# A window-attention and gated-expert kernel: the output product of tiles 3 to 8 by seven block products as well

## Chip, core and metric

The kernel runs on one core of one Trainium2 chip. The metric is the device time of one execution in microseconds (us); the table below gives it as the median of three runs. Everything said of single instructions comes from one further execution, which the hardware profiler recorded. TensorE (PE) does the matmuls, VectorE (DVE) and ScalarE (ACT) work on PSUM and SBUF, GpSimd (POOL) on SBUF, and SyncE (SP) issues nearly all DMA transfers.

## What is computed

Attention over a window of 64 positions, and behind it a gated expert layer:

```python
scores = q @ k.T / sqrt(64), masked to 0 <= i - j < 64     # 8 batches, 8 heads, 576 positions, head size 64
x = (softmax(scores) @ v), heads side by side              # 4608 tokens x 512
xn = x / sqrt(mean(x*x) + 1e-6) * rms_g
g, val = xn @ w_gate, xn @ w_val                           # 512 -> 1536
out = (silu(g) * val) @ w_out                              # 1536 -> 512
```

All tensors are float32. To keep nearly that precision on TensorE, each operand of the expert layer is split into a high and a low half of 16 bits, and each product is three matmuls: high by high, high by low, low by high.

## The kernel before

The 4608 tokens are nine tiles of 512 (`TT`), t = 0 to 8. The hidden width of 1536 is six chunks c of 256 (`NC`, `WC`). Tiles 0 to 2 multiply plainly. From tile 3 (`FIRST7`) on the gate and value products of a chunk are made by a seven-product scheme (Strassen and Winograd's): tokens, features and columns are halved, and sums and differences of the quarters of the weights and of x are multiplied, seven block products in place of eight (`product`, L976). One block product is 12 matmuls of 128x256 (L992). The weight sums are made once by `prepare` (L910), are kept in DRAM (`sevens`), and are streamed back for each chunk by `load_sevens` (L968, L974) into one of three SBUF buffers, `wts[r % 3]`.

`seventh` (L1026) runs product p and hands the accumulator on: ACT copies it away (`snap`, L1007), DVE adds a kept copy (L1045, L1048, L1052), and `quad` (L1010) makes the gated values of one quarter: a tanh on ACT (L1016), two DVE operations on 128x256 (L1017, L1018). When both halves of a row of quarters are there, ACT writes the high half (L1023) and POOL, or DVE for the last chunk, the low half (L1024).

The output product of these tiles is plain: `chunk_out` (L1126) multiplies, for 128 tokens k and chunk c, six matmuls of 128x512 through `three` (L845 to L847). One such unit is an `out_unit`, 24 units make a tile, and `store` (L1133) scales the result of six units on ACT (L1135) and writes it out (L1148).

The order is written by hand in slots. A slot is one block product or one output unit on TensorE; a tile has `SHORT` = 66 slots, 42 products (places 7c + `PLACE[p]`) and 24 units, which begin at slot 42 and fill the free slots, two of them in the next tile. `at_slot(when, part)` puts any other work into the order at a fractional slot, and each engine and DMA queue runs its instructions strictly in that order. The attention of batch b runs during tile b - 1, up to tile 6, at the offsets `SCORES`, `VALUES` and so on: scores of a head pair on TensorE (L395), masks on DVE (L408), exponentials on ACT (L411), scaling on POOL (L366), a transposition through DRAM by SP (L374, L380) and DVE (L383), values on TensorE (L526). Normalising (L788) and the sums and splits of x (`combine`, L814) follow. Tiles 7 and 8 have no attention beside them.

From tile 1 on the eight PSUM banks are one pool: each new tile takes the next bank in turn (`any_bank`, L86).

Of the kernel before, what the change touches and what calls it, by code (L numbers as in the profile page):

```python
# [7 lines left out]

# [17 lines left out]
P = 128  # L26
# [14 lines left out]
LT0, LV0 = 1.4, 2.6  # L41
SCORES, VALUES = (-14, -4, 8, 21), (12, 22, 34, 47)
LOAD, MASK, EXP, SUM, SCALE, AWAY, BACK, TURN = -6, (0.3, 0.5), (1.3, 0.9), 9.7, 10, 12.5, 16, 22
ROOTS, FIRST, SECOND, PIECE = 50.5, 52.5, 61, 0.85
FIRST7 = 3
PLACE = {1: 0, 5: 2, 2: 3, 6: 4, 3: 6, 7: 8, 4: 12}
LONG, SHORT = 72, 66
PREP, PREP_EVERY, PREP_PIECE = 3, 9.6, 0.9
ST = 2 * NBLK * P - 32
NRB = B  # L50
S1, LK1, LV1, LQ1 = [-2, 1, 3, 6, 10, 12.5, 15.5, 19], 2.5, 6, 7
# [11 lines left out]
def tile_window_attention_moe(  # L63
# [22 lines left out]
    def any_bank(name):  # L86
        return shared["banks"].tile([P, TT], F32, tag="bank", name=name)
# [168 lines left out]
    def in_scale(c):  # L256
# [18 lines left out]
        nc.gpsimd.tensor_scalar(h_inv[:, c : c + 1], s[:, 1, 0:1], 2.0**-6, s[:, 1, 1:2], ALU.mult, ALU.mult)  # L275
# [137 lines left out]
    def scores_of_pair(n, qk, first):  # L413
# [121 lines left out]

    def attention(b):
# [21 lines left out]
        def moves(hp):  # L558
            n = b * NPAIR + hp

            def turned():
                p, m, _ = whole.pop(n)
                turn(p, m)
                soft[hp, 0] = soft[hp, 1] = p

            return (
                (SCALE, lambda: scale(whole[n][0], whole[n][2])),
                (AWAY, lambda: away(n, whole[n][0])),
                (BACK, lambda: back(n, whole[n][1])),
                (TURN, turned),  # L570
            )
# [4 lines left out]
        def values(hp, g, xp=None):  # L576
            n = b * NPAIR + hp
            vv = pairs[hp][1]
# [12 lines left out]
            nc.scalar.copy(xb[:, hp, a:z], xp[:, : z - a])  # L591
            if g == 0:
                return
# [4 lines left out]
        def squares(hp):  # L598
            xb, ssq = norm["x"], norm["ssq"]
            x2 = pairs[hp][0] if hp else ssq  # L600
            x2e = E("X2E", "a" * 8)[b * NPAIR + hp] if b < 2 else "a"
# [5 lines left out]
        def add(hp):  # L607
            ssq = norm["ssq"]
            if hp:
                e = nc.vector if (E('ADD', 'ppvppv')[3 * b + hp - 1] == 'v' if b < 2 else hp == NPAIR - 1) else nc.gpsimd  # L610
                e.tensor_tensor(ssq, ssq, pairs[hp][0], ALU.add)

        def roots():
            norm["r"] = inverse_roots(b, norm["ssq"])
# [33 lines left out]
    def at_slot(when, part):  # L648
        if when < 0:
            at_step(half_steps + when / 2, part)  # L650
        else:
            timed.append((when, len(timed), part))
            timed.sort(key=lambda e: e[:2])

    def attention_slots(b):
# [9 lines left out]
        def normal(piece, when):  # L665
            for i, part in enumerate(normal_parts(piece)):
                at_slot(when + PIECE * i, part)

        for hp in range(NPAIR):
            s, v = t0 + SCORES[hp], t0 + VALUES[hp]  # L670
            early_by = 14 if b == TB and hp < 2 else -LOAD
            at_slot(s - early_by, partial(load_queries, hp))
            at_slot(s - early_by, partial(load_keys, hp))
# [5 lines left out]
        at_slot(t0 + ROOTS, roots)  # L679
        at_slot(t0 + FIRST, partial(normal, 0, t0 + FIRST))  # L680
        at_slot(t0 + SECOND, partial(normal, 1, t0 + SECOND))

    def first_batch():
# [12 lines left out]
        LT, LV = [LT0] * 8, [LV0] * 8  # L696
# [28 lines left out]
    def inverse_roots(b, ssq):  # L725
# [13 lines left out]
        inverse_root(m, r, w, tot[:, :nst])  # L739
        return r  # L740
# [30 lines left out]
    def normalise(b, xb, r, piece):  # L771
# [104 lines left out]
    def group_in(t, c, i, m, bank):  # L876
# [17 lines left out]
        nc.vector.scalar_tensor_tensor(th, a, 2.0**-41, th, ALU.mult, ALU.mult)  # L894
# [11 lines left out]
    RIGHT = {1: "11", 2: "21", 5: "t1", 6: "t2", 3: "22", 7: "t3", 4: "t4"}  # L906
    sevens = [dram.tile([P, 14 * TT], F16, name=f"sevens{c}") for c in range(NC)]
    HT = TT // 2

    def prepare(c, i):  # L910
# [40 lines left out]
        def away(j):  # L951
            nc.sync.dma_start(out=out_of[:, 2 * TT * (2 * i + j) : 2 * TT * (2 * i + j + 1)], in_=halves[j])
# [6 lines left out]
    def block(p, i, j):  # L959

        if p in SUMS:
            return 2 * TT * (2 * i + j) + HT * SUMS[p]
        at = 8 * TT + 3 * TT * i
        return at + (2 * TT + HT * j if p == 4 else TT * j + HT * (p - 1))

    SUMS = {6: 0, 7: 1, 3: 2, 5: 3}

    def load_sevens(r):  # L968
# [3 lines left out]
        dst = wts[r % 3].rearrange("p i a n -> p (i a n)")  # L972
        for a, z in ((0, 8 * TT), (8 * TT, 14 * TT)):
            nc.sync.dma_start(out=dst[:, a:z], in_=sevens[r % NC][:, a:z])  # L974

    def product(t, c, p, acc, first):  # L976
# [3 lines left out]
        for i in range(2):  # L980
            ws = []
            for j in range(2):
                o = block(p, i, j)
                w = wt[4 * (r % 3) + o // 2048].rearrange("p a n -> p (a n)")
                ws.append(w[:, o % 2048 : o % 2048 + HT].rearrange("p (k f) -> p k f", k=2))
# [19 lines left out]
    def snap(src, t, c, p):  # L1005
        d = wt[11][:, 1, :].bitcast(F32) if p == 5 else late.tile([P, TT], F32, tag=f"s{p}", name=f"s{p}_{t}_{c}")
        nc.scalar.copy(d, src)  # L1007
        kept[c, p] = d

    def quad(t, c, i, half, acc):  # L1010

        if (c, "th", i) not in kept:
            kept[c, "th", i] = wk.tile([P, TT], F32, tag="t2k", name=f"th_{t}_{c}_{i}", bufs=T2K), []
        th, done = kept[c, "th", i]
        cols = th[:, half * HT : (half + 1) * HT]
        nc.scalar.activation(cols, acc[:, :HT], AF.Tanh, scale=th_scale[:, c : c + 1])  # L1016
        nc.vector.scalar_tensor_tensor(cols, cols, 1.0, acc[:, :HT], ALU.add, ALU.mult)  # L1017
        nc.vector.scalar_tensor_tensor(cols, acc[:, HT:], 2.0**-41, cols, ALU.mult, ALU.mult)  # L1018
        done.append(half)
        if len(done) == 2:  # L1020
            kept.pop((c, "th", i))
            hh, hl = hs[t, c][:, 0, i, :], hs[t, c][:, 1, i, :]
            nc.scalar.copy(hh, th)  # L1023
            (nc.vector if c == NC - 1 else nc.gpsimd).tensor_tensor(hl, th, hh, ALU.subtract)  # L1024

    def seventh(t, c, p):  # L1026

        if p == 1:
            hs[t, c] = wk.tile([P, 2, 2, TT], F16, tag="f4k", name=f"h_{t}_{c}", bufs=F4K)
# [6 lines left out]
        if p == 1:  # L1036
            kept[c, "x"] = acc
            snap(acc, t, c, 1)
        elif p == 5:
            kept[c, "w"] = acc  # L1040
            snap(acc, t, c, 5)
        elif p == 6:
            snap(acc, t, c, 6)
        elif p == 2:
            nc.vector.tensor_tensor(acc, acc, kept.pop((c, 1)), ALU.add)  # L1045
            quad(t, c, 0, 0, acc)
        elif p == 3:
            nc.vector.tensor_tensor(acc, acc, kept.pop((c, 6)), ALU.add)  # L1048
            quad(t, c, 0, 1, acc)
        elif p == 7:  # L1050
            w = kept[c, "w"]
            nc.vector.tensor_tensor(w, acc, kept.pop((c, 5)), ALU.add)  # L1052
            quad(t, c, 1, 1, w)
        else:
            quad(t, c, 1, 0, acc)
            load_sevens(NC * (t - FIRST7) + c + 3)
# [9 lines left out]
    def outs_of(t):  # L1066
        last = NC - 1
        order = [(0, c) for c in range(last)] + [(1, c) for c in range(last - 1)] + [(0, last), (1, last - 1), (1, last)]
        order += [(k, c) for k in range(2, TT // P) for c in range(NC)]
        return [(tile_start(t) + (NC + 1) * last + 7, t, k, c) for k, c in order]  # L1070
# [3 lines left out]
    def out_unit(t, k, c):  # L1074
        if t == NT - 1 and k == TT // P - 1:
            if c == 0:
                for e in range(2):
                    es = slice(e * DM // 2, (e + 1) * DM // 2)
                    po = any_bank(f"po_{t}_{k}_{e}")[:, es]
                    for c in range(NC):  # L1080
                        chunk_out(po, t, c, k, c == 0, c == NC - 1, es)
                    store(po, t, k, es)
            return
# [7 lines left out]
    def rest_of_tiles():  # L1091
# [5 lines left out]
        for t in range(1, FIRST7):  # L1097
            for c in range(NC):
# [5 lines left out]
                if t == FIRST7 - 1 and c % 2:  # L1104
                    at_slot(now, partial(load_sevens, c // 2))
# [200 lines left out]
```

## Time and profile before

| | |
|---|---|
| time, median of 3 runs | 1003.25 us (1003.04 to 1003.25) |
| profiled execution | 1004.02 us, of which 1002.1 us from the first to the last instruction |
| granted TensorE clock, mean | 0.986 |
| busy: PE, DVE, ACT, POOL | 971.0, 578.4, 498.9, 330.3 us |
| moved by DMA | 171.74 MB, mean 171 GB/s |

A group's row has the source line, the engine, the operation, what it writes and reads, the shapes and the count; then the busy time and the mean duration of one; then the idle time of the engine just before these instructions and what ended it. A row of the windows has the stretch, its length, and then the busy time of PE, of PE's weight loads (PEld), DVE, ACT and POOL with the counts of instructions, the granted clock, the share of DMA and GB/s. Matmuls overlap in the records, so that the cadence from start to start says what one costs, and not its mean duration.

### The profile page before, as it was taken

The numbers are of one execution on the slowest core, as the hardware profiler recorded it, in microseconds if no ns is written. First come the engines' busy times: TensorE is split into PE (matmuls) and PEld (weight loads), VectorE is DVE, ScalarE is ACT, GpSimd is POOL, SyncE is SP. The second block draws the span as 40 slices with busy tenths as digits, with TensorE's granted clock in tenths as the row PEclk, the third lists the DMA queues.
The fourth block names the chain that finished last, engine by engine and source line by source line (L and its number), as shares of the span: only waits on it lengthen the run. The fifth ranks groups of instructions, "written<-read, shape, count | busy, mean of one in ns | idle before, by whom it ended". The sixth has DMA issues, their size and how long they took to land.

```text
span 1002.1 us, 20583 instructions
## 1 busy us (share of the span) xinstructions
PE 971.0 (97%) x7853; PEld 632.1 (63%) x7853; DVE 578.4 (58%) x1647; ACT 498.9 (50%) x1303; POOL 330.3 (33%) x391
## 2 busy tenths in 40 slices
PE   7789989999999999999999999999999999999998
PEld 5544534555444455488758875887588758857875
DVE  6688958247775676456555655565456535522640
ACT  5567887245424543466436643664376425523531
POOL 3336643143514442433234322432243213200210
PEclk9989988999999999999999999999999999999999
DMA  7635651317345966277745883678358614631501
GB/s 286 188 114 171 214 180 36 112 52 185 107 130 165 272 219 215 82 256 255 273 127 201 262 273 104 228 260 274 108 194 288 226 33 136 212 126 64 179 2 43
DMA packets 78242, 171.74 MB, mean 171 GB/s; under 512 B 25792, under 2 KB 38336, under 8 KB 73536
## 3 DMA queue, kind: packets, MB, share of 16 engines
q1 hardware_dynamic: 77568, 169.24, 52.5%
q8 instruction: 62, 1.02, 0.4%
q10 hardware_dynamic: 576, 1.18, 0.3%
q14 instruction: 36, 0.29, 0.1%
HBM read 135.79 MB, written 34.60 MB: 170 GB/s over the span
## 4 chain that ended last, share of the span: by engine, by line
PE 70%; DMA 1%; ACT 0%; SPq 0%; DVE 0%; issue 0%; DVEq 0%; ACTq 0%
PE a L992 33%; PE po L845 8%; PE po L847 8%; PE po L846 8%; PE xp L526 3%; PE sc L395 2%; PE pg L845 1%; PE pv L845 1%; PE pv L847 1%; PE pv L846 1%; PE pg L847 1%; PE pg L846 1%; PE rb L760 1%; PE tot L729 1%; DMA kv<-kv 1%; PE s L395 0%
## 5 line engine op out<-in xcount | busy, mean ns | idle before, releaser
L992 PEld LDWEIGHTS <-wt 128*128 128x128 f16 x3024 | 292.7, 98 | 42.0 <-issue 1.4
L992 PE MATMUL a<-xn,wt 128*128 128x256 f16 x1728 | 205.2, 273 | 0.0
L845 PE MATMUL po<-wt,h 128*128 128x512 f16 (+1 forms) x436 | 162.9, 374 | 0.0
L847 PE MATMUL po<-wt,h 128*128 128x512 f16 (+1 forms) x436 | 162.8, 373 | 0.0
L846 PE MATMUL po<-wt,h 128*128 128x512 f16 (+1 forms) x436 | 162.8, 373 | 0.0
L992 PE MATMUL a<-wt,wt 128*128 128x256 f16 x1104 | 133.7, 273 | 0.0
L1024 POOL TENSOR_TENSOR h<-th,h 128x512 f16<-128x512 f32 x60 | 69.4, 1157 | 189.6 <-ACT h L1023 177.1
L1017 DVE SCALAR_TENSOR_TENSOR th<-th,a 128x256 f32<-128x256 f32 x144 | 60.5, 420 | 107.4 <-ACT th L1016 107.4
L1016 ACT ACTIVATE th<-a,hsc 128x256 f32<-128x256 f32 x144 | 67.9, 472 | 91.3 <-DVE a L1045 43.4
L1135 ACT ACTIVATE ot<-po,hsc 128x512 f32<-128x512 f32 (+1 forms) x37 | 25.0, 675 | 148.7 <-PE po L847 128.6
L411 ACT ACTIVATE pm<-pm,st 128x128 f32<-128x128 f32 (+1 forms) x216 | 84.0, 390 | 7.2 <-DVE st L408 7.0
L1023 ACT CAST h<-th 128x512 f16<-128x512 f32 x72 | 44.5, 618 | 74.9 <-DVE th L1018 74.9
L366 POOL TENSOR_TENSOR pm<-pm,st 128x512 f32<-128x512 f32 (+1 forms) x72 | 59.8, 858 | 50.7 <-DVE st L442 37.1
L847 PEld LDWEIGHTS <-h 128*128 128x128 f16 x436 | 42.7, 98 | 48.6 <-issue 0.2
L845 PEld LDWEIGHTS <-h 128*128 128x128 f16 x436 | 43.6, 100 | 44.4 <-issue 1.7
L846 PEld LDWEIGHTS <-h 128*128 128x128 f16 x436 | 42.7, 98 | 42.1
L828 POOL TENSOR_TENSOR xn<-xb,xn 128x192 f16<-128x192 f32 (+7 forms) x33 | 24.0, 741 | 126.0 <-ACT xn L827 125.7
L1018 DVE SCALAR_TENSOR_TENSOR th<-a,th 128x256 f32<-128x256 f32 x144 | 61.1, 424 | 4.9
L395 PE MATMUL sc<-kv,q 64*64 64x128 f32 (+1 forms) x1056 | 54.7, 295 | 7.6 <-DMA q<-q 4.9
L896 POOL TENSOR_TENSOR h<-th,h 128x512 f16<-128x512 f32 x30 | 38.4, 1279 | 71.2 <-ACT h L895 61.0
L1045 DVE TENSOR_TENSOR a<-a,s 128x512 f32<-128x512 f32 x36 | 25.0, 695 | 61.9 <-PE a L992 61.5
L845 PE MATMUL pg<-xn,wt 128*128 128x512 f16 x144 | 55.5, 386 | 2.4 <-ACT wt L232 1.9
(175 smaller groups left out, 1670.8 us busy)
## 6 DMA issues: line engine op xcount, KB each, us to landing
wt<-sevens SPq DMA_DIRECT2D x36, 1024.0 KB, 5.9
wt<-sevens SPq DMA_DIRECT2D x36, 768.0 KB, 5.0
kv<-kv SPq DMA_DIRECT2D x28, 608.0 KB, 5.6
via<-pm SPq DMA_DIRECT2D x96, 144.0 KB, 2.6
pm<-via SPq DMA_DIRECT2D x24, 576.0 KB, 3.9
q<-q SPq DMA_DIRECT2D x28, 288.0 KB, 3.8
kv<-kv SPq DMA_DIRECT2D x56, 128.0 KB, 5.7
out<-ot SPq DMA_DIRECT2D x27, 256.0 KB, 2.1
```

The lines of the kernel that those rows point to most:

```text
L366: nc.gpsimd.tensor_tensor(p[:, :ks, us, :], p[:, :ks, us, :], r, ALU.mult)
L395: nc.tensor.matmul(out.rearrange("p (n c) -> p n c", c=D), lhsT=qt[hd, j * D : (j + 1) * D], rhs=halves[hd, :1, :] if j == 0 else halves[h ...
L411: nc.scalar.activation(part, part, AF.Exp, bias=low, scale=-1.0, accum_out=total)
L845: nc.tensor.matmul(acc, lhsT=lh, rhs=rh, start=first, stop=False)
L846: nc.tensor.matmul(acc, lhsT=lh, rhs=rl, start=False, stop=False)
L847: nc.tensor.matmul(acc, lhsT=ll, rhs=rh, start=False, stop=last)
L992: nc.tensor.matmul(acc[:, i * HT : (i + 1) * HT], lhsT=ws[l][:, kt, :], rhs=b[:, m, kt, :], start=at_start, stop=kt == 1 and j == 2, skip_ ...
L1016: nc.scalar.activation(cols, acc[:, :HT], AF.Tanh, scale=th_scale[:, c : c + 1])
L1017: nc.vector.scalar_tensor_tensor(cols, cols, 1.0, acc[:, :HT], ALU.add, ALU.mult)
L1018: nc.vector.scalar_tensor_tensor(cols, acc[:, HT:], 2.0**-41, cols, ALU.mult, ALU.mult)
L1023: nc.scalar.copy(hh, th)
L1024: (nc.vector if c == NC - 1 else nc.gpsimd).tensor_tensor(hl, th, hh, ALU.subtract)
```

## The change

For tiles 3 to 8 the output product goes the way of the gate product: tokens, hidden columns and output columns are halved, and seven products are made, each over all six chunks. A unit is one product p over two chunks, 12 matmuls of 128x256; 21 units make a tile, and `SHORT` becomes 63. The gated values need sums now, four per chunk, made on DVE (`hidden_sums`), and their high and low halves are made of four operands a, b, c, d (`hidden_halves`; a, b and c 128x512, d 128x256), the high ones on ACT and the low ones all on POOL. The sums of `w_out` are made by `prepare_out` for each chunk in tiles 2 and 3, kept in DRAM (`outer`) and loaded four times a tile by `load_outer`. As c and these blocks need room, `load_sevens` has two buffers in place of three, and loads each in three pieces as products 2, 3 and 4 free them; `prepare` writes to DRAM in 10 pieces per matrix and chunk in place of 6. Three accumulators of the output product are snapped and three added to, as with the gate product, and a quarter of the output (`quarter_out`) is scaled and stored in two halves.

The second part: a new PSUM tile takes the bank that has been free longest, from a list to which `done_with` gives a bank back where its last reader is issued. And the offsets of the order are retuned: a list for batches up to 3 and one for later ones (`WHEN`), own times for each `prepare`, and `seventh` no longer issues its DVE and ACT work at once but 0.4 to 2 slots apart. Work of attention is the same.

```diff
-LONG, SHORT = 72, 66
+LONG, SHORT = 72, 63
+OUT_FROM = 42
+OUT_ORDER = ((1, 0), (1, 1), (5, 0), (5, 1), (2, 0), (2, 1), (1, 2), (5, 2)) + tuple((p, u) for p in (6, 3, 7) for u in range(3)) + ((2, 2), (4, 0), (4, 1), (4, 2))
+PREPARE_OUT = [(117.64, 0.7), (127.0, 0.7), (135.37, 0.7), (145.0, 0.7), (154.0, 0.7), (163.0, 0.7)]
...
     def any_bank(name):
-        return shared["banks"].tile([P, TT], F32, tag="bank", name=name)
+        k = shared["free"].pop(0)
+        shared[name] = k
+        return shared["banks"].tile([P, TT], F32, tag=f"bank{k}", name=name)
+
+    def done_with(name):
+        if name in shared:
+            shared["free"].append(shared.pop(name))
...
+    def prepare_out(c):
+        def whole_of(i):
+            r.append(wk.tile([P, TT], F32, tag="t2k", name=f"ro{i}_{c}", bufs=T2K))
+            nc.vector.tensor_tensor(r[i], w[:, 0, i], w[:, 1, i], ALU.add)
+        def sums(k):
+            (b11, b12), (b21, b22) = ([x[:, a * HT : (a + 1) * HT] for a in range(2)] for x in r)
+            if k == 0:
+                nc.vector.tensor_tensor(b11, b11, b12, ALU.subtract)
+                nc.vector.tensor_tensor(b12, b22, b12, ALU.subtract)
+            else:
+                nc.vector.scalar_tensor_tensor(b22, b11, -1.0, b22, ALU.mult, ALU.subtract)
+                nc.vector.tensor_tensor(b21, b21, b22, ALU.add)
+        def half(j, d):
+            if j == 0:
+                nc.scalar.copy(h, r[d])
+            else:
+                (nc.vector if d else nc.gpsimd).tensor_tensor(l, r[d], h, ALU.subtract)
...
+        a, z = (2 * TT * x for x in GROUPS[group])
+        nc.sync.dma_start(out=flat[r % 2][:, a:z], in_=sevens[r % NC][:, a:z])
...
+    def load_outer(p):
+        n = NC * TT
+        nc.sync.dma_start(out=outer_block(p), in_=outer[:, PLACED_OUT[p] * n : (PLACED_OUT[p] + 1) * n])
...
+    def outer_product(t, p, acc, cs, first, last):
+        for c in cs:
+            l, r = outer_left(t, c, p), outer_right(c, p)
+            for sub in range(2):
+                for j, (x, y) in enumerate(((0, 0), (0, 1), (1, 0))):
+                    nc.tensor.matmul(
+                        acc[:, sub * HT : (sub + 1) * HT],
+                        lhsT=l[:, x, sub * P : (sub + 1) * P],
+                        rhs=r[:, y, :],
...
+    def quarter_out(src, t, r, e):
+        nc.scalar.activation(ot, src, AF.Copy, scale=out_scale)
+        for sub in range(2):
+            for a, z, tok in runs_of(t, 2 * r + sub):
+                nc.sync.dma_start(out=out[tok : tok + z - a, e * HT : (e + 1) * HT], in_=ot[a:z, sub * HT : (sub + 1) * HT])
...
+    def hidden_sums(t, c, k):
+        if k == 0:
+            nc.vector.scalar_tensor_tensor(u[:, :HT], a21, -1.0, a22, ALU.mult, ALU.subtract)
+        elif k == 1:
+            nc.vector.tensor_tensor(a21, a11, a21, ALU.subtract)
+        elif k == 2:
+            nc.vector.tensor_tensor(u[:, HT:], a11, u[:, :HT], ALU.add)
+        else:
+            nc.vector.tensor_tensor(u[:, HT:], a12, u[:, HT:], ALU.add)
+
+    def hidden_halves(t, c, which, j):
+        if j == 0:
+            nc.scalar.copy(hi, src)
+        else:
+            nc.gpsimd.tensor_tensor(lo, src, hi, ALU.subtract)
```

More of the change, by code (lines that the diff above doesn't have):

```diff
@@ L7 @@
 from functools import partial
+from itertools import count
 import concourse.bass as bass
@@ L534, in attention_values @@
         return xp
+    chain = {}
     def attention(b):
@@ L564, in turned, with step, run @@
                 soft[hp, 0] = soft[hp, 1] = p
[L566 to L571, printed above, removed]
+            when = WHEN[b > FIRST7]
+            def step(k, part):
+                def run():
+                    assert chain.get(n, 0) == k, (n, k, chain.get(n, 0))
+                    chain[n] = k + 1
+                    part()
+                return run
+            return tuple((at, step(k, part)) for k, (at, part) in enumerate((
+                (when["scale"], lambda: scale(whole[n][0], whole[n][2])),
+                (when["away"][hp], lambda: away(n, whole[n][0])),
+                (when["back"][hp], lambda: back(n, whole[n][1])),
+                (when["turn"][hp], turned),
+            )))
         def to_keys(hp, g):
@@ L608, in add @@
             ssq = norm["ssq"]
+            chain["add", b] = chain.get(("add", b), 0) + 1
+            assert chain[b * NPAIR + hp] == 6 and chain["squares", b] >= chain["add", b]
             if hp:
@@ L613, in roots @@
         def roots():
+            assert chain["add", b] == NPAIR
             norm["r"] = inverse_roots(b, norm["ssq"])
@@ L678, in attention_slots @@
             at_slot(v + 2.2, partial(add, hp))
-        at_slot(t0 + ROOTS, roots)
-        at_slot(t0 + FIRST, partial(normal, 0, t0 + FIRST))
-        at_slot(t0 + SECOND, partial(normal, 1, t0 + SECOND))
+        at_slot(t0 + when["roots"], roots)
+        for piece, name in enumerate(("first", "second")):
+            at, every = when[name]
+            at_slot(t0 + at, partial(normal, piece, t0 + at, every))
     def first_batch():
@@ new lines, in seventh, with later, add @@
+        if p in (1, 5):
+            kept[c, "x" if p == 1 else "w"] = acc
+        if p in (1, 5, 6):
+            at_slot(done, partial(snap, acc, t, c, p))
+            return
+        def later(parts, start):
+            for n, part in enumerate(parts):
+                at_slot(start + HALVES * n, part)
+        def add(to, name):
+            nc.vector.tensor_tensor(to, acc, kept.pop((c, name)), ALU.add)
+        mul = done + TANH
+        if p == 2:
+            at_slot(done, partial(add, acc, "s1"))
+            at_slot(mul, partial(timed_quad, mul, t, c, 0, 0, acc))
@@ L1066, in outs_of @@
     def outs_of(t):
[L1067 to L1070, printed above, removed]
+        return [(tile_start(t) + OUT_FROM, t, p, u) for p, u in OUT_ORDER]
     pos = {}
     def out_unit(t, k, c):
[L1075 to L1083, printed above, removed]
         if c == 0:
```

292 lines of the change are left out of this document (198 added, 94 removed).

## The prediction

> **What bounds the kernel now.** I read the page first: busy times, then the chain that ended last by engine.
>
> ```profile
> span 1002.1 us, 20583 instructions
> PE 971.0 (97%) x7853; PEld 632.1 (63%) x7853; DVE 578.4 (58%) x1647; ACT 498.9 (50%) x1303; POOL 330.3 (33%) x391
> PE 70%; DMA 1%; ACT 0%; SPq 0%; DVE 0%; issue 0%; DVEq 0%; ACTq 0%
> ```
>
> TensorE is nearly full, and the chain is TensorE. Next the windows of the stages that the change touches: the product stage of tiles 3, 5 and 7, and the output stage of tile 5.
>
> ```profile
> 427.00:490.70 63.70, 63.70 (x685) 54.33 (x683) 38.61 (x109) 39.63 (x114) 23.65 (x27) 1.00 0.79 257
> 625.60:690.80 65.20, 65.20 (x692) 54.97 (x690) 40.67 (x111) 40.40 (x113) 27.21 (x30) 1.00 0.73 245
> 690.80:725.60 34.80, 34.80 (x269) 18.79 (x267) 18.26 (x73) 12.15 (x44) 6.39 (x12) 1.00 0.50 163
> 823.30:879.60 56.30, 56.30 (x501) 48.71 (x499) 31.07 (x61) 29.98 (x57) 17.63 (x16) 1.00 0.51 162
> ```
>
> TensorE is busy in every microsecond, at granted clock 1.00. DVE is at 62% in a product stage beside attention (40.67 of 65.20), ACT at 62%, POOL at 42%. The table of who waited shows all that TensorE waited for another engine or a transfer from 200 us to the end:
>
> ```profile
> PE tot L729 <- DVE ssq L611: 1.7, 1, 1.7
> PE pg L845 <- ACT ot L1135: 0.6, 1, 0.6
> PE s L395 <- DMA kv<-kv: 0.4, 1, 0.4
> ```
>
> So what is taken from TensorE in tiles 3 to 8 comes off the time, one for one, while the other engines keep up; and banks given out otherwise have at most the 0.6 us (a bank's reader) to win.
>
> **The saving on TensorE.** Tile 7 has no attention, and the chain in order of time gives its cadence:
>
> ```profile
> 823.36 1.31 PE a L992 x12
> 831.19 47.16 PE a L992 x432
> 884.84 1.31 PE a L992 x12
> 909.46 1.31 PE a L992 x12
> ```
>
> 36 products of 12 matmuls take 47.16 us, 1.31 us each. From the end of the last product (884.84 + 1.31 = 886.15) to the first of tile 8 (909.46) there are 18 output units, 23.31 us, 1.295 us each. Check: 42 x 1.31 + 24 x 1.295 = 86.1 us, and from 823.36 to 909.46 it is 86.10. After the change 21 units have the shape of a product, so I cost them at 1.31: 27.5 us in place of 31.1, 3.57 us less in each of six tiles, **21.4 us** in all. A wide matmul costs 1.295 / 6 = 216 ns, and two narrow ones 2 x 1.31 / 12 = 218 ns, so of the three slots saved (3.9 us a tile) 0.3 us goes to the shorter shape; that is in the sum.
>
> **What the other engines get.** Rows for the added operations, from the groups:
>
> ```profile
> L935 DVE SCALAR_TENSOR_TENSOR r<-r,r 128x256 f32<-128x256 f32 x12 | 7.8, 654 | 0.2
> L936 DVE TENSOR_TENSOR r<-r 128x256 f32<-128x256 f32 x12 | 7.6, 634 | 0.4
> L938 DVE TENSOR_TENSOR r<-r,r 128x256 f32<-128x256 f32 x12 | 8.5, 706 | 0.2
> L939 DVE TENSOR_TENSOR r<-r,r 128x256 f32<-128x256 f32 x12 | 6.4, 536 | 0.4
> L927 DVE TENSOR_TENSOR r<-wt 128x512 f32<-128x512 f16 x24 | 19.1, 801 | 0.0
> L949 DVE TENSOR_TENSOR lo<-r,hi 128x512 f16<-128x512 f32 x12 | 9.1, 760 | 0.3 <-ACT hi L947 0.3
> L1048 DVE TENSOR_TENSOR a<-a,s 128x512 f32<-128x512 f32 x36 | 25.0, 696 | 4.0 <-PE a L992 3.9
> L1024 POOL TENSOR_TENSOR h<-th,h 128x512 f16<-128x512 f32 x60 | 69.4, 1157 | 189.6 <-ACT h L1023 177.1 <-POOL h L1024 6.6 <-issue 3.9
> L1023 ACT CAST h<-th 128x512 f16<-128x512 f32 x72 | 44.5, 618 | 74.9 <-DVE th L1018 74.9
> ```
>
> The four sums of a chunk are operations of the kind of L935 to L939, 128x256 with both inputs in SBUF: mean (654 + 634 + 706 + 536) / 4 = 632 ns. But this mean hides two populations:
>
> ```profile
> L935 DVE SCALAR_TENSOR_TENSOR r<-r,r x12: 414/426/1418, 223.3 to 381.8; 128x256 f32<-128x256 f32 x12
> L938 DVE TENSOR_TENSOR r<-r,r x12: 414/426/1508, 224.2 to 383.6; 128x256 f32<-128x256 f32 x12
> 381.92 1.34 POOL L896 TENSOR_TENSOR h<-th,h 128x512 f16<-128x512 f32 x1 [0.95 <-ACT h L895]
> 382.28 1.26 DVE L936 TENSOR_TENSOR r<-r 128x256 f32<-128x256 f32 x1
> ```
>
> Median 426 ns, up to 1508 ns; and the timeline shows a long one, 1.26 us, that began 0.36 us after a POOL operation and ended 0.28 us after it. A DVE sum that meets POOL is held. [...]
>
> Per tile, **DVE**: 24 sums at 632 ns, 15.2 us; three additions (L1048) 2.1 us; less two low halves that go to POOL. Some 20 sums lie in the product stage (those of the last chunk come behind it), 12.6 us. Tiles 4 to 6: 40.67 + 12.6 = 53.3 of 65.2 us, 82%. DVE keeps pace until the mean sum reaches (65.2 - 40.67) / 20 = 1.23 us. Tiles 7 and 8 I take as free: the window of tile 7 holds the same operations per chunk without attention's.
>
> Tile 3 is the tight one, since three of the six `prepare_out` (slots 145 to 163 and on) fall into it. Each is two of L927, four sums, one of L949 on DVE: 1.60 + 2.53 + 0.76 = 4.9 us, three 14.7. So 38.61 + 12.6 + 14.7 = 65.9 us in a stage of 63.7 us, 103%; at the 426 ns median for the sums it is 38.61 + 8.5 + 12.2 = 59.3, 93%. A strict queue this full makes TensorE wait for banks and for the additions before product 4 (three slots of slack). Bounds: nothing, to 65.9 - 63.7 + 4 of idle that a queue with waits keeps, some 6 us. I take **2.0 us**. For tiles 4 to 6 the bounds are 0 (today's 62% costs nothing) and 1.5 us each (a sum held as in the longest row at a bad moment); I take 0.5 each, **1.5 us**. The other three `prepare_out` lie in tile 2, where this window has room for 14.7 us more:
>
> ```profile
> 325.00:427.00 102.00, 101.64 (x719) 50.60 (x718) 62.46 (x173) 43.32 (x124) 40.40 (x44) 1.00 0.63 196
> ```
>
> **ACT** gains two casts (L1023's 618 ns at most) a chunk, 7.4 us a tile; **POOL** two subtractions of at most 1157 ns and the last chunk's two, 16.2 us: 47.8 and 43.4 of 65.2 us even if all lay in the stage. Both have room.
>
> **DMA and SP's queue.** The loads of gate sums move the same bytes in three pieces. New are four loads of 768 KB a tile, 3.1 MB. Tile 5 moves 245 x 65.2 + 163 x 34.8 = 21.6 MB in 100 us; 24.7 MB in 96.4 us is 257 GB/s, just what the product stage of tile 3 moves today with TensorE full. So bandwidth costs nothing. The order matters more: with two buffers the last pieces for the second chunk wait for product 4 of the output, slot 68 of the tile before, behind that quarter's stores, which wait for ACT; product 6 needs them at slot 74. That leaves five slots, 6.55 us.
>
> ```profile
> wt<-sevens SPq DMA_DIRECT2D x36, 768.0 KB, 5.0
> sevens<-hi SPq DMA_DIRECT2D x12, 256.0 KB, 2.3
> L1135 ACT ACTIVATE ot<-po,hsc 128x512 f32<-128x512 f32 (+1 forms) x37 | 25.0, 675 | 148.7 <-PE po L847 128.6 <-issue 19.7 <-ACT s L1007 0.4
> L1148 SPq DMA_DIRECT2D out<-ot x45: 316/350/598, 183.6 to 998.8; - x45
> ```
>
> The scaling takes 0.68 us, two to four stores 0.35 us each to issue, the load 0.35 us to issue and, at 512 KB, between 2.3 and 5.0 us to land: 4.0 to 7.4 us. Late by at most 0.9 us at each of five boundaries, probably by nothing, since attention's scores lie between; I take 0.1 each, **0.5 us**. The more numerous pieces of `prepare` queue ahead of attention's loads in tile 1, at the same 0.3 to 0.6 us of issue; those loads are issued six slots early, which covers them.
>
> The operands of the last chunk: product 7 ends at slot 44, and output product 1 needs operand a half way through slot 50, 8.5 us later. The chain is one addition, tanh and two multiplications of about 0.45 us each, three sums, one cast, two subtractions: 0.70 + 1.35 + 1.9 + 0.62 + 2.31 = 6.9 us. Covered, with 1.6 us to spare; a further POOL operation ahead would use 1.16 of that.
>
> **The tail.** The last records are
>
> ```profile
> 997.96 0.27 PE L847 MATMUL po<-wt,h 128*128 128x256 f16 x1
> 998.33 0.47 ACT L1135 ACTIVATE ot<-po,hsc 128x256 f32<-128x256 f32 x1 [3.46 <-PE po L847]
> ```
>
> Today the last piece is half wide: one scaling of 0.47 us and one store. Then it is a full 128x512, 0.68 us, and two stores issued one after the other: 0.2 + 0.35, **0.5 us** more.
>
> Retuned offsets move attention by a slot or less; by the rows of who waited, what they can win is the 2.7 us above, what they can lose I bound by the same; I take zero.
>
> **Sum.** 21.4 - 2.0 - 1.5 - 0.5 - 0.5 = 16.9 us less. The profiled execution's 1004.02 us becomes 987.1; it stood 0.77 us above the median, so against the median of 1003.25 I forecast **986.3 us**, 1.7% faster. 0.2%, 2 us, is about what a measurement of this kernel can tell from no change.
>
> **The rivals.** *Clean*: DVE absorbs all, and only the tail costs: 1003.25 - 20.9 = 982.3 us. For it: between tanh and multiplication DVE gets other work now, and by the table of who waited, for 625 to 690 us, DVE idles there today (row below), so that it can take more work than its busy share says. Against it: 103% in tile 3. Chance 0.24.
>
> ```profile
> DVE th L1017 <- ACT th L1016: 15.3, 20, 2.1
> ```
>
> *DVE late in tile 3 and after, but not ruinous*: with mean m of the sums and `prepare_out` scaled alike (14.7 / 0.632 = 23.3 m), tile 3 overflows by 38.61 + 43.3 m - 63.7 us; at m = 0.8 that is 9.5 us, with the 2.5 us of the other terms 993.9 us. For it: POOL gets half as much work again, so more sums meet one. Chance 0.14.
>
> *Slower: DVE becomes the bound*, in the product stages, by sums held behind POOL. It eats the whole saving from 43.3 m - 25.1 = 20.4, m = 1.05 us (tiles 4 to 6 begin to add only at 1.23). At 1.2 us tile 3 loses 26.9 and the tail 0.5, 1009.2 us. The rows' mean of 632 ns, at today's POOL, speaks against. Chance 0.06. [...]
>
> *Weights late*: the two-buffer loads miss by a landing of 5.0 instead of 2.3 us, plus SP's queue, at each of five boundaries, 2.7 us each, 13.5 us beyond the forecast's other terms: 999 us. Chance 0.06.
>
> *It does not do what it says*: narrow units run slower than products in a row, at the 1.42 us that a product between attention's matmuls takes:
>
> ```profile
> 443.31 1.42 PE a L992 x12
> ```
>
> 21 x 1.42 = 29.8, only 1.3 us a tile, 7.8 us, with the losses 1000 us. Its spread reaches no change, and I count it there. Chance 0.02.
>
> **Numbers.** The forecast's own case has 0.48; its upper ends (6, 4.5, 4.5 and 0.5 us) would all at once make 997.3, which I leave out. Range 981 to 996: at the low end clean, with half of the 2.7 us of waits gone, at the high end the late DVE with 2 us of the loads; outside lie the slow case, the weights and the slow units, 0.14. Faster by over 0.2%: 0.92; within 0.2%: 0.02; slower: 0.06.
>
> **What would show it.** Right: tiles 7 and 8 repeat every 82.5 us; units of 12 at 1.31 us; TensorE's idle time in tile 3's product stage near 2 us with DVE as its releaser, above 85% busy; sums bimodal at 0.43 and above 1 us. Wrong: TensorE waiting for `wt<-sevens` at the start of a tile's second chunk, sums with a mean over 0.8 us, or a period of tile 5 above 97.5 us.

## The result and the profile after

The changed kernel takes **991.04 us** (median, 989.8 to 992.64) against 1003.25 us: ratio 0.9877, 95% interval 0.986 to 0.9894. In a later group of runs it took 988.03 us against 1002.82 us, ratio 0.9852 (0.9831 to 0.9874). It is faster, as forecast, by 12 to 15 us in place of 16.9. Two of the seven executions of one later run, `e_stall_short`, were slow (1627 and 3370 us) and stay out of its median.

First the cadence. In the chain of the changed kernel (a product is line L1141 there, an output unit L1084), the first products of tiles 5 to 8 and the run of 36 products in tile 7 stand at

```profile
627.03 1.31 PE a L1141 x12
722.93 1.31 PE a L1141 x12
816.51 1.31 PE a L1141 x12
824.37 47.16 PE a L1141 x432
899.04 1.31 PE a L1141 x12
```

Tile 7 takes 899.04 - 816.51 = 82.53 us in place of 86.10: the 3.57 us of the forecast to the last digit. Tile 6 takes 93.58, tile 5 95.90 us. Taking the start of each tile's first matmul from the records (the 505th product matmul begins tile 4, and so on) gives a table by tile for every profile, in us:

| profile | to tile 1 | 1 | 2 | 3 | 4 | 5 | 6 | 7 | 8 and tail |
|---|---|---|---|---|---|---|---|---|---|
| before | 212.1 | 108.6 | 107.2 | 97.4 | 100.2 | 100.0 | 97.8 | 86.1 | 92.8 |
| changed | 211.3 | 107.0 | 110.3 | 101.7 | 96.6 | 95.9 | 93.6 | 82.5 | 89.7 |
| changed, again | 210.5 | 107.0 | 110.3 | 102.1 | 96.7 | 96.3 | 93.6 | 82.7 | 89.7 |
| `e_roots` | 210.6 | 107.0 | 107.5 | 101.4 | 96.3 | 96.1 | 93.6 | 82.6 | 89.4 |
| `e_kv` | 210.5 | 107.0 | 110.3 | 101.9 | 96.5 | 97.0 | 94.6 | 82.5 | 89.7 |
| `e_s3` | 209.1 | 107.0 | 110.3 | 98.9 | 96.1 | 96.8 | 93.6 | 82.6 | 89.4 |
| `e_noprep` | 210.0 | 107.0 | 109.2 | 93.9 | 97.6 | 96.3 | 93.6 | 82.6 | 89.7 |
| `e_qk` | 209.2 | 107.0 | 110.3 | 99.8 | 96.3 | 96.3 | 94.1 | 82.5 | 89.9 |
| `e_best` | 210.7 | 107.0 | 107.5 | 101.8 | 96.8 | 96.9 | 94.0 | 82.5 | 89.4 |
| `e_early` | 210.9 | 107.0 | 117.3 | 97.6 | 97.8 | 96.9 | 93.6 | 82.6 | 89.4 |
| `e_pool` | 210.9 | 107.0 | 107.5 | 100.6 | 98.0 | 96.2 | 94.0 | 82.5 | 89.7 |
| `b_firstfree` | 207.5 | 110.3 | 107.6 | 97.4 | 100.2 | 100.0 | 97.7 | 86.1 | 92.8 |
| `e_stall_short` | 210.6 | 107.0 | 110.3 | 101.2 | 96.6 | 96.1 | 93.6 | 86.6 | 93.7 |
| `e_stall_long` | 211.1 | 107.0 | 110.3 | 101.6 | 97.4 | 96.1 | 95.9 | 93.8 | 102.6 |

Tiles 4 to 8 gain 3.1 to 4.2 us each, tile 1 gains 1.6 us, and **tiles 2 and 3 lose 3.1 and 4.3 us**, where the forecast had tile 2 unchanged and tile 3 gaining 1.6. The rows of the product stages of tiles 3, 4, 5 and 7 have DVE as the third busy time. It is at 76 and 78% in tiles 4 and 5, where the forecast had 82%, and at 80% in tile 3, where it had 93 to 103%. TensorE idles mostly in tile 3:

```profile
428.50:494.00 65.50, 60.69 (x638) 51.62 (x636) 52.59 (x142) 42.09 (x120) 32.89 (x36) 0.95 0.80 256
531.00:594.00 63.00, 62.60 (x687) 54.58 (x685) 47.86 (x139) 43.78 (x123) 35.92 (x42) 1.00 0.87 291
627.00:691.00 64.00, 64.00 (x702) 56.01 (x700) 49.92 (x145) 45.13 (x125) 37.19 (x43) 1.00 0.86 290
824.30:880.00 55.70, 55.70 (x513) 49.86 (x512) 38.98 (x87) 31.63 (x64) 26.47 (x25) 1.00 0.63 207
```

In tile 5 DVE is 78% busy and TensorE waits for nothing; in tile 3 DVE has 80%, hardly more over the whole stage, TensorE idles 4.8 us, and the granted clock is 0.95. The table of who waited, from 200 us on, names the waits:

```profile
PE s L412 <- DMA kv<-kv: 2.9, 2, 2.5
PE tot L769 <- DVE ssq L647: 2.6, 2, 2.1
PE xp L546 <- DVE th L1171: 2.3, 1, 2.3
```

Each of the three long ones can be followed in the timeline. **First**, at 391 us in tile 2, the matmuls of the sums of squares (L769) wait 2.1 us for the last addition, L647, which stands on DVE behind the sums of `prepare_out` (L1024 to L1028):

```profile
391.92 0.42 DVE L1027 SCALAR_TENSOR_TENSOR ro<-ro,ro 128x256 f32<-128x256 f32 x1
392.38 0.42 DVE L1028 TENSOR_TENSOR ro<-ro 128x256 f32<-128x256 f32 x1
392.72 0.75 DVE L647 TENSOR_TENSOR ssq<-ssq,kv 128x576 f32<-128x576 f32 x1
393.53 1.28 PE L769 MATMUL tot<-one,ssq 128*128 128x1 f32 x10 [2.09 <-DVE ssq L647]
```

**Second**, in tile 3, the scores of the third head pair wait 2.5 us for keys that were issued at 430.94, 2.4 us after the tile's first product, and landed 8 us later. The DMA engines were nearly full meanwhile (the figure before the last):

```profile
434.00:438.00 4.00, 2.58 (x24) 2.05 (x22) 2.25 (x5) 1.54 (x4) 2.14 (x3) 1.00 0.97 287
```

In the kernel before, the same keys were issued 1.9 us after the tile's first product, took 5.5 us and landed 0.5 us ahead of the scores. **Third**, at 463 us, values wait 2.3 us for a bank, whose last reader L1171 stands on DVE behind a `prepare_out` addition; that addition waited for its buffer, which a store still held; and the store stood in SP's queue (L1041) behind a load of keys (L350), which had waited 6.0 us for its own buffer:

```profile
456.83 0.33 SPq L350 DMA_DIRECT2D kv<-kv  x1
458.45 0.56 SPq L1041 DMA_DIRECT2D outer<-hi_o  x1
463.12 1.48 DVE L1019 TENSOR_TENSOR ro<-wt 128x512 f32<-128x512 f16 x1 [0.58 <-DMA outer<-hi_o]
465.53 1.04 PE L546 MATMUL xp<-pm,kv 64*64 64x64 f32 x20 [2.26 <-DVE th L1171]
```

And each of the three is dearer than its length. Behind the first one the granted clock (third figure from the end) is

```profile
393.00:397.00 4.00, 3.47 (x18) 2.10 (x19) 2.36 (x10) 0.88 (x2) 2.64 (x2) 0.82 0.21 66
397.00:401.00 4.00, 4.00 (x18) 2.00 (x17) 1.67 (x5) 0.00 (x0) 0.00 (x0) 0.76 0.38 113
```

The clock records of the trace show one stretch of 3.41 us at half rate there, and one behind each of the other two, 10.2 us at half rate in tiles 2 and 3, where the kernel before has none: some 1.7 us of lost matmul time each. Idle time and half clock together account for tile 3: its length, less TensorE's idle time in it, less half of its time at half clock, is 93.1 to 94.3 us in the changed kernel, in its repetition and in all eight variants that follow from `e_roots` to `e_pool`. In the changed kernel that is 101.7 less 4.8 and 3.4, or 93.5 us.

### The profile page after: what moved, and what is told of

Same layout as the page of the kernel before. It is cut to its first block, busy times and chain, and to the rows that moved or that the text cites. A ratio compares the mean times of both kernels' runs of the same rounds, so it can differ in the third digit from the quotient of the medians.

```text
span 988.5 us, 22548 instructions
## 1 busy us (share of the span) xinstructions
PE 950.5 (96%) x8465; PEld 693.4 (70%) x8465; DVE 663.8 (67%) x1839; ACT 545.6 (55%) x1404; POOL 420.3 (43%) x481
## 2 busy tenths in 40 slices
DMA packets 106653, 193.89 MB, mean 196 GB/s; under 512 B 28208, under 2 KB 65072, under 8 KB 106544
## 4 chain that ended last, share of the span: by engine, by line
PE 88%; DMA 4%; DVE 4%; ACT 3%; issue 1%; SPq 1%; ACTq 0%; DVEq 0%
PE a L1141 32%; PE o L1084 15%; PE xp L546 5%; PE sc L412 4%; PE pv L888 3%; PE po L888 3%; PE po L890 3%; PE pg L888 3%; PE po L889 3%; PE pv L890 3%; PE pv L889 3%; PE pg L890 3%; PE pg L889 3%; DMA kv<-kv 2%; DMA wt<-sevens 1%; PE tr L527 1%
## 5 line engine op out<-in xcount | busy, mean ns | idle before, releaser
L1141 PEld LDWEIGHTS <-wt 128*128 128x128 f16 x3024 | 294.2, 98 | 37.9 <-issue 0.8
L1141 PE MATMUL a<-xn,wt 128*128 128x256 f16 x1728 | 203.1, 273 | 0.0
L1210 POOL TENSOR_TENSOR wt<-u,wt 128x512 f16<-128x512 f32 x72 | 66.2, 920 | 152.6 <-ACT wt L1208 98.6
L1141 PE MATMUL a<-wt,wt 128*128 128x256 f16 x1044 | 127.1, 273 | 0.0
L1210 POOL TENSOR_TENSOR h<-th,h 128x512 f16<-128x512 f32 x72 | 85.5, 1189 | 45.8 <-ACT h L1208 44.1
L1084 PE MATMUL o<-wt,h 128*128 128x256 f16 x864 | 101.1, 273 | 0.0
L1084 PEld LDWEIGHTS <-h 128*128 128x128 f16 x864 | 84.1, 98 | 10.6 <-issue 1.0
L1239 DVE TENSOR_TENSOR a<-a,s 128x512 f32<-128x512 f32 x72 | 50.2, 697 | 46.1 <-PE a L1141 43.6
L1084 PEld LDWEIGHTS <-wt 128*128 128x128 f16 x648 | 63.5, 99 | 7.2
L941 POOL TENSOR_TENSOR h<-th,h 128x512 f16<-128x512 f32 x30 | 38.2, 1273 | 65.2 <-ACT h L940 55.4
L1171 DVE SCALAR_TENSOR_TENSOR th<-a,th 128x256 f32<-128x256 f32 x144 | 61.1, 424 | 5.0
L425 DVE CUSTOM_DVE_ANT_0 pm<-sc,blocked 128x128 f32<-128x128 f32 x192 | 49.3, 283 | 15.4 <-PE sc L412 15.3
L888 PE MATMUL pv<-xn,wt 128*128 128x512 f16 x144 | 55.8, 388 | 0.7 <-DVE th L936 0.7
L890 PE MATMUL pv<-xn,wt 128*128 128x512 f16 x144 | 55.9, 388 | 0.0
L889 PE MATMUL pv<-xn,wt 128*128 128x512 f16 x144 | 55.8, 387 | 0.0
L888 PEld LDWEIGHTS <-wt 128*128 128x128 f16 x296 | 29.2, 99 | 36.8 <-issue 2.4
```

The lines of the kernel that those rows point to most:

```text
L888: nc.tensor.matmul(acc, lhsT=lh, rhs=rh, start=first, stop=False)
L889: nc.tensor.matmul(acc, lhsT=lh, rhs=rl, start=False, stop=False)
L890: nc.tensor.matmul(acc, lhsT=ll, rhs=rh, start=False, stop=last)
L1084: nc.tensor.matmul(acc[:, sub * HT : (sub + 1) * HT], lhsT=l[:, x, sub * P : (sub + 1) * P], rhs=r[:, y, :], start=first and c == cs[0] an ...
L1141: nc.tensor.matmul(acc[:, i * HT : (i + 1) * HT], lhsT=ws[l][:, kt, :], rhs=b[:, m, kt, :], start=at_start, stop=kt == 1 and j == 2, skip_ ...
L1171: nc.vector.scalar_tensor_tensor(cols, acc[:, HT:], 2.0**-42, cols, ALU.mult, ALU.mult)
```

## The experiments

Theory A, formed from this: three separate stalls, each with a half-clock stretch. Theory B, the forecast's own: DVE is too full in tile 3. Medians of whole runs vary by 3 us for the same kernel. Part of that lies ahead of tile 1, where all variants of the changed kernel have the same code: it takes them 209.1 to 211.3 us, with 17 to 27 us at half clock before 200 us. So the table by tile carries the verdicts, from one profile of each.

**The changed kernel again** (`after_again`, 988.03 us).

> The changed kernel as it is, beside the others of this group. Theory A (three stalls before and in tile 3, each with a stretch at half clock behind it): TensorE idles some 2 us before the matmuls of L769 of tile 2, some 2.5 us before the scores of the third head pair in tile 3 and some 2 us before values in tile 3, at much the same places in another profile, and tiles 7 and 8 repeat every 82.5 us. Rival B (DVE too full in tile 3's product stage, as forecast): the idle is spread over tile 3's product stage in small pieces, DVE above 90% busy. Time by both: about 991 us.

The same three stalls at the same places (2.1, 3.1 and 2.3 us), the second now put down to DVE (the keys landed 0.1 us before it ended). The places are the kernel's, not one execution's. B's small scattered pieces are not there.

**First stall** (`e_roots`, 987.77 us, ratio 0.9845, 0.9823 to 0.9866).

```diff
-PREPARE_OUT = [(117.64, 0.7), (127.0, 0.7), (135.37, 0.7), ...
+PREPARE_OUT = [(121.6, 0.7), (129.0, 0.7), (136.5, 0.7), ...
```

> The first three prepare_out begin later (slots 121.6, 129 and 136.5 in place of 117.64, 127 and 135.37), so that the last addition to the sums of squares in tile 2 goes ahead of them on DVE; nothing else. Theory A: the 2.1 us of idle before L769 in tile 2 go, and the half clock behind them, 2.1 + 1.7 = 3.8 us; some comes back if prepare_out now delays normalising: 3 us less, 988 us. Rival B: tile 2 does not matter, and the sums now crowd into tile 3's beginning: same time or up to 2 us more.

```profile
PE tot L769 <- DVE ssq L647: 1.0, 1, 1.0
```

The wait falls from 2.1 to 1.0 us, the half clock behind it is gone, and tile 2 takes 107.5 in place of 110.3 us: 2.8 us from 1.1 us of wait. So the order on DVE, `prepare_out` ahead of one addition, cost 1.1 us of wait. The 1.0 us that is left is not its doing: the addition now waits 1.3 us for a square on ACT, and it does so too in the run below that leaves `prepare_out`'s work out. There the same wait of 1.0 us was followed by a half-clock stretch, and tile 2 took 109.2 us, 1.7 us more at the same length of wait. The median gains less than its interval can tell.

**Second stall** (`e_kv`, 990.75 us, 0.9877, 0.9863 to 0.9891).

```diff
-... 'keys': [-6, -6, -5.27, -6], ...
+... 'keys': [-6, -6, -8.27, -6], ...
```

> For batches from 4 on the keys and values of the third head pair are loaded 3 slots (3.9 us) sooner; nothing else. Theory A: they land before slot 7 of tile 3, the 2.5 us of idle and the half clock behind it go, about 4 us less, 987 us. Rival C (DMA bandwidth is short at the start of tile 3, not the order): the load takes as much longer to land as it starts sooner, or the weights' loads become late: less than 1.5 us gained.

```profile
PE s L412 <- DMA q<-q: 2.7, 1, 2.7
```

A miss: the stall stays, and the transfer named is now the queries, which stand behind the keys in SP's queue. It left open whether the queue or the bandwidth was short.

**Both transfers sooner** (`e_qk`, 989.38 us, 0.9878, 0.9858 to 0.9899).

```diff
-            sooner = 8 if b == TB and hp < 2 else 0
+            sooner = 8 if b == TB and hp < 2 else 3 if b == FIRST7 + 1 and hp == 2 else 0
```

> For batch 4 alone, queries, keys and values of the third head pair are loaded 3 slots (3.9 us) sooner. In the run that moved the keys alone, the queries, now behind them in SP's queue, became what the scores waited for. Theory A (the scores of tile 3 wait for transfers that are issued late): the idle of some 2.5 us and the half clock behind it go, tile 3 takes 101.9 - 2.5 - 1.7 = 97.7 us, tiles 1, 2 and 4 to 8 as they were. Rival C (DMA bandwidth): the transfers land no sooner, tile 3 stays above 100 us.

The second stall is gone, with its half clock. The keys, issued 1.0 us sooner behind queries that went 3.2 us sooner, took 4.5 us to land in place of 8.1; so against rival C an earlier place in the order was enough, though the DMA engines were at 0.95 in these 4.5 us. But tile 3 falls only to 99.8 us, not to theory A's 97.7, as a new wait of 1.1 us for DVE appears at 453 us, and the third stall stays at 2.2 us.

**Third stall** (`e_s3`, 987.09 us, 0.9844, 0.9823 to 0.9865).

```diff
-            nc.sync.dma_start(out=ends, in_=halves[j]...
+            (nc.sync if j else nc.scalar).dma_start(out=ends, in_=halves[j]...
```

> The stores of the high halves of the sums of w_out go through ACT's queue in place of SP's, where one of them stands behind a load of keys that waits 6 us for its buffer; nothing else. Theory A: DVE no longer waits for that store's buffer in tile 3, the values' matmuls come in time, about 2.3 + 1.7 = 4 us less if the wait was the cause; if DVE's order of work (prepare_out ahead of the quads) or POOL's hold on it is the larger part, 1 to 2 us remain of the idle. Rival B: within 1 us of the changed kernel.

The third stall is 1.2 us in place of 2.3, without a half clock, and tile 3 takes 98.9 us, 2.8 less. So the store behind the load was about half of it. The profile puts the rest down to DVE (L1171); what in DVE's order makes it late was not tested.

**Without prepare_out's work** (`e_noprep`, 981.6 us, 0.9787, 0.9766 to 0.9808).

```diff
-            partial(whole_of, 0), partial(whole_of, 1), partial(sums, 0), partial(sums, 1), ...
+        return [lambda: None] * 8 + [partial(plain, 0), partial(plain, 1)]
```

> prepare_out makes no sums and no halves: it stores the halves of w_out as they are, at the same slots and with the same transfers; so four of the seven output products multiply other numbers. Theory A: the stalls before L769 and before the values go, the late keys stay: 7 to 8 us less than the changed kernel, about 983.5 us, and 979.5 if the keys come in time because SP's queue is freer. Rival B (DVE too full in tile 3): 4 us less, all of it from tile 3.

```profile
PE s L412 <- DVE th L1172: 0.6, 1, 0.6
```

That is all that TensorE waits for in tile 3 now. Tile 3 takes 93.9 us, 3.45 less than before the change, though the transfers are as many and as large (193.87 MB for 193.89). The keys come in time too. They are issued 2.4 us after the tile's first product, as in the changed kernel, but land in 6.1 us in place of 8.1; why they took less time is not shown. So all of tile 3's loss, near 8 us, comes with the work of `prepare_out`; 1.0 us of that moves to tile 4, where scores wait 1.5 us for keys. Tile 2 keeps 2.0 us of its loss, against theory A. Rival B had the place and A the number.

**The three repairs together** (`e_best`, 988.21 us, 0.9859, 0.9844 to 0.9874).

> Three changes at once: the first three prepare_out begin later, the high halves of their sums are stored through ACT's queue, and queries and keys of the third head pair of batch 4 come 3 slots sooner. Theory A: tile 2 takes 107.5 us, tile 3 about 95 us (94 without prepare_out's work at all, and 1 us for the third stall, whose rest is DVE's order), the others as they were: 991 less 2.8 and less 6.5, about 981 us, faster than the kernel before and the changed one. Rival B (DVE full): tile 3 stays at 98 us or above.

Tile 2 as expected, 107.5 us. Tile 3 does not improve at all, 101.8 us: the waits for transfers are nearly gone, and in their place stand

```profile
PE xp L546 <- DVE th L1171: 2.2, 1, 2.2
PE a L1141 <- DVE th L1171: 1.4, 1, 1.4
PE a L1141 <- DVE a L1239: 1.1, 1, 1.1
```

with DVE (9.53 and 9.43 of 10 us) full in the two stretches where it happens:

```profile
440.00:450.00 10.00, 9.79 (x101) 8.24 (x99) 9.53 (x35) 7.38 (x24) 1.70 (x4) 1.00 0.90 279
450.00:460.00 10.00, 8.59 (x112) 7.16 (x110) 9.43 (x18) 7.30 (x20) 7.42 (x10) 1.00 0.96 311
```

Theory A falls here as a sum of three independent costs: the stalls covered for one another. In the changed kernel too the 80% of the whole stage hide 20 us at 93%, around the third stall:

```profile
450.00:460.00 10.00, 10.00 (x114) 8.56 (x112) 9.35 (x22) 7.98 (x21) 8.15 (x9) 1.00 0.67 245
460.00:470.00 10.00, 7.74 (x107) 6.03 (x105) 9.21 (x25) 4.23 (x11) 3.58 (x4) 0.86 1.00 322
```

In `e_noprep` the fullest 20 us of tile 3 have 83%. From this theory D: DVE full over 20 us, with transfers that come last by chance.

**prepare_out away from tile 3** (`e_early`, 993.27 us, 0.9909, 0.9894 to 0.9924).

```diff
-PREPARE_OUT = [(117.64, 0.7), (127.0, 0.7), (135.37, 0.7), (145.0, 0.7), (154.0, 0.7), (163.0, 0.7)]
+PREPARE_OUT = [(90.0, 0.7), (100.0, 0.7), (108.0, 0.7), (121.6, 0.7), (129.0, 0.7), (136.5, 0.7)]
```

> All six prepare_out in tile 2 (slots 90, 100, 108, 121.6, 129, 136.5), none in tile 3; nothing else, so transfers of keys and queries are as in the changed kernel. The combined run had mended two waits for transfers and left tile 3 at 101.8 us, with TensorE waiting for DVE instead, DVE 94 to 95% busy from 440 to 460 us; without prepare_out's work tile 3 took 93.9 us. Theory D, formed from that (DVE full for 20 us in tile 3 by prepare_out beside the new sums; the transfers were only the wait that came last): tile 3 takes 94 to 96 us, tile 2, whose DVE now has 12 us more, 107 to 109 us; in all 5 to 8 us less than the changed kernel, 981 to 984 us. Theory A (late keys of their own): the keys' stall stays, tile 3 about 98 us. Rival E: the work costs in tile 2 what it cost in tile 3, tile 2 above 113 us, no gain.

Rival E holds: tile 2 takes 117.3 us, 7 more, with waits of 2.8 and 3.1 us and two half-clock stretches, one of 3.41 and one of 6.83 us, DVE being full where the first of these waits is,

```profile
361.00:373.00 12.00, 9.22 (x70) 4.76 (x68) 11.03 (x17) 3.24 (x6) 6.44 (x7) 0.92 0.61 164
```

and tile 3 takes 97.6 us, with the keys' stall of 2.6 us back alone, as A said. So in tile 3 the late keys cost by themselves, without a full DVE. They are not free of `prepare_out`, though: its last two stores come out at the start of tile 3, ahead of the keys, which are issued 3.6 us after the first product in place of 2.4.

**Work from DVE to POOL** (`e_pool`, 988.2 us, 0.9854, 0.9829 to 0.9879).

```diff
-            nc.vector.tensor_tensor(r[i], w[:, 0, i], w[:, 1, i], ALU.add)
+            (nc.gpsimd if c > 2 else nc.vector).tensor_tensor(r[i], w[:, 0, i], w[:, 1, i], ALU.add)
...
-                (nc.vector if d else nc.gpsimd).tensor_tensor(l, r[d], h, ALU.subtract)
+                (nc.vector if d and c < 3 else nc.gpsimd).tensor_tensor(l, r[d], h, ALU.subtract)
```

> As the combined run (first three prepare_out later; queries and keys of the third head pair of batch 4 three slots sooner; all stores on SP again), and for the three prepare_out of tile 3 the two whole sums and one low half go from DVE to POOL, which is half idle there: 3 x (0.8 + 0.8 + 0.8 to 1.6) = 7 to 10 us less on DVE. Theory D (tile 3 loses both to late keys and to a full DVE, and mending one shows the other): both are gone, tile 2 takes 107.5 us, tile 3 94 to 97 us, in all 980 to 984 us, faster than the kernel before and the changed one. Rival F: POOL's work delays the low halves, or holds DVE's sums longer (two inputs in SBUF), and tile 3 stays at 100 us or above.

Rival F holds: tile 3 takes 100.6 us. The waits for DVE shrink to 1.1 and 0.4 us, and keys are late again. The longest wait, 2.3 us, is for those of the fourth head pair. They were issued sooner than in the changed kernel (26.7 us after the tile's first product in place of 28.3) and took 7.5 us to land in place of 4.7. Earlier in tile 3, SP's queue stood 7.5 us at a store whose low half POOL had not made, and the stores of the transposition stood behind it; that this made the keys late is not shown.

```profile
SPq L1041 <- POOL lo_o L1037: 7.5, 1, 7.5
```

No version tried beats the changed kernel by more than the runs can tell, apart from the one that leaves the work out.

**Banks alone** (`b_firstfree`, the kernel before with first free: 1001.59 us, 0.9998, 0.9984 to 1.0012).

> The kernel before with one part of the change alone: PSUM banks given out by first free. By the prediction and theory A: within 1 us of before, as TensorE waited 0.6 us for banks in all. Rival: banks in turn made hidden waits, and first free alone gains 2 us or more; or first free gives a bank whose reader is still queued, and loses as much.

No difference, as forecast.

**What a wait costs** (`e_stall_short`, 997.5 us, 0.9955, 0.9942 to 0.9969; `e_stall_long`, 1015.13 us, 1.0117, 1.0091 to 1.0144).

```diff
+    def stall(k, n):
+        b = any_bank(f"st{k}")
+        nc.tensor.matmul(b[:, :P], lhsT=ident, rhs=ident, start=True, stop=True)
+        z = late.tile([P, P], F32, tag="stall", name=f"stz{k}")
+        nc.vector.tensor_copy(z, b[:, :P])
+        for _ in range(n):
+            nc.vector.tensor_scalar(z, z, 1.0, None, ALU.mult)
+        nc.tensor.matmul(b[:, P : 2 * P], lhsT=z, rhs=ident, start=True, stop=True, skip_group_check=True)
...
```

> Six waits of about 1 us are put into tiles 7 and 8, where TensorE is otherwise never idle: a small matmul, two DVE operations behind it and a matmul that needs them. It tells what a wait costs beyond its own length. Theory A: waits of 1 us leave the clock at full rate, so the time grows by the sum of the waits, about 6 x 1.3 = 8 us with the added matmuls, and the granted clock in tiles 7 and 8 stays 1.00. Rival: any idle time halves the clock, 6 x 1.7 us more.

> The same with nine DVE operations in each of the six waits, about 2.3 us each. Theory A: each is followed by one stretch of 3.41 us at half clock, 1.7 us more: 6 x (2.5 + 1.7) = 25 us; rows show clock below 1.00 behind each. Rival (the half clock behind the three stalls was no effect of the idle time): 15 us and clock 1.00.

The six short waits came to 0.6 us each, and tiles 7 and 8 grew by 8.1 us, the clock at 1.00 throughout; 4.2 us of that are not wait but come with the added matmuls. The long ones, 2.5 us each (14.9 us), made tiles 7 and 8 24.2 us longer, and only three of the six were followed by a half-clock stretch. The sum closes: 14.9 + 4.2 + 3 x 1.7 = 24.2 us. Two of the long waits, the first without a half-clock stretch behind it:

```profile
833.00:838.00 5.00, 2.52 (x23) 2.14 (x22) 3.46 (x13) 0.34 (x1) 0.00 (x0) 1.00 0.89 310
838.00:842.00 4.00, 4.00 (x39) 3.59 (x37) 2.69 (x8) 2.64 (x6) 2.10 (x2) 1.00 0.44 141
855.00:859.50 4.50, 2.02 (x18) 1.66 (x16) 3.43 (x13) 0.01 (x1) 0.00 (x0) 0.98 0.53 175
859.50:863.50 4.00, 4.00 (x24) 3.00 (x23) 1.87 (x6) 2.07 (x5) 1.16 (x1) 0.59 0.00 0
```

So theory A is half right: of six waits of 2.5 us three were followed by no stretch. Where such waits fell is in the last section.

## Why the prediction was right, and where not

The forecast was 986.3 us in a range of 981 to 996; measured were 991.0 and, again, 988.0.

The range held in part by luck. By tile, tiles 2 and 3 came out some 9 us worse than forecast, and tile 1 and tiles 4 to 8 some 4.5 us better.

- **The saving on TensorE** held exactly: 3.57 us in tile 7, 3.1 to 4.2 in tiles 4 to 8. Units of 12 matmuls take 1.31 us. No slower units, no late weights: the weight loads wait 0.2 us for `wt<-sevens` in all.
- **The sums** were over-priced: by groups they take 463, 424, 418 and 553 ns, 464 on average for the forecast's 632. Of the 144, 16 took over 600 ns, up to 1.3 us, and each of the 16 ran beside a POOL operation; eleven are the fourth sum of a chunk. Of the sums that met a POOL operation 16 of 21 were that long (in the kernel before, 13 of 20 on L935 to L939), the other five took 0.42 to 0.53 us; of those that met none, not one took over 427 ns. The slower rival needed 1.05 us.

```profile
L1184 DVE SCALAR_TENSOR_TENSOR u<-th,th x36: 412/419/776, 448.2 to 959.3; 128x256 f32<-128x256 f32 x36
L1192 DVE TENSOR_TENSOR u<-th,u x36: 419/425/1309, 453.0 to 963.4; 128x256 f32<-128x256 f32 x36
```

- **Tile 3, "I take 2.0 us"** is the term that was mis-sized: it measured 7.7 to 8 us (101.7 against the 93.9 without `prepare_out`'s work), more than its upper bound of some 6, of which 4 us of idle were the author's estimate. The place and the culprit were right, `prepare_out`; the way was only half right. The stage was to overflow, DVE at 93 to 103%, and TensorE to wait for DVE alone. In fact DVE had 80% over the stage and was nearly full (93%) for 20 us only; of 4.8 us of idle time 2.5 were a wait for keys; and half clock cost 3.4 us more. So the sign that the prediction set for itself, idle time near 2 us with DVE as its releaser and DVE above 85%, failed.
- **"So bandwidth costs nothing"** was weighed over a whole tile in the same way. At the start of tile 3 the DMA engines were nearly full (0.97 from 434 to 438 us), and the keys took 8.1 us to land in place of 5.5 before: the second stall.
- **"The other three prepare_out lie in tile 2, where this window has room"** failed: a window of 102 us had room, the 4 us around the roots' wait had not (DVE 3.86 of 4.00 us busy from 389 to 393 us): 2.1 us of wait and a half-clock stretch, 3.1 us in all against before. Of the wait 1.1 us are `prepare_out`'s.
- **The price of a wait** was missing from every term: the forecast charged waits at their length.
- **Tiles 4 to 6, 0.5 us each**, were lost at most in tile 4: 0.4 us of idle there, none in 5 and 6. Tiles 5 and 6 gained 4.1 and 4.2 us, more than the 3.57, for which no run here gives a reason. **The tail, 0.5 us**: tile 8 gains 0.4 us less than tile 7. **Retuned offsets, zero**: tile 1 gained 1.6 us, of which 1.2 are the wait for the sums of squares, 0.5 us in place of 1.7.

Open is how tile 3's 8 us divide between DVE's order, SP's queue and the crowded DMA engines: every mended wait let another one come last, and a version with all of these stores off SP's queue was not tried.

## What to carry to other kernels

Room on an engine, and on the DMA engines, is to be read over short stretches and not over a stage: here 80% of DVE over 65 us held 20 us at 93%, and DMA at 0.80 over the same stage held 4 us at 0.97. Work put in "where there is room" brings its stores too, and in `e_pool` a store that waited 7.5 us for its data held what stood behind it in SP's queue. Where several waits stand close together, mending the one that came last can move the loss to the next (tile 3 took 101.8 us in `e_best`, 101.7 before the repairs); leave the suspected work out first, to see what all of it costs.

## What the hardware showed that was not expected

In the fourteen profiles a wait of TensorE mostly cost either its length or 1.7 us more, and the difference went with where the wait fell in steps of 3.41 us. The half-clock stretches of one profile begin at multiples of 3.41 us from each other (in the changed kernel at 395.54, 439.91 and 467.22 us, 13 and 8 steps apart), and from 200 us on each lasts one or two such steps, mostly one; a stretch that the end of the record cuts short is not counted. The following leaves out the second step of the two that lasted two. Cutting every idle time over 0.25 us of TensorE after 200 us at these steps: each step with 1.86 to 2.97 us of idle was followed by one at half clock; of those with less than 1.6 us only some at L769 were, where ten one-column matmuls follow (three times, from 0.99 us on); in between, seven of eight. So the 2.48 us of wait at 834 us in `e_stall_long`, which the steps cut into 1.24 and 1.23, is followed by no half clock. Nor is a wait of 1.73 us, cut into 1.0 and 0.73, in the kernel before at 287 us; the same 1.73 us in one step cost a stretch in `b_firstfree`, whose tile 1 is 1.7 us longer. Why the steps count so is not shown.
